# Linear attention and a gated long convolution on one core: the last output blocks sent one PSUM bank at a time over three queues, and the last 162 steps in a new order

## The chip, the cores and the metric

The kernel runs on one core of a Trainium2 chip. The metric is the device time of one execution in microseconds (us). Matrix products run on TensorE (PE, with PEld for its weight loads), elementwise work on VectorE (DVE), ScalarE (ACT) and GpSimd (POOL). The queues of SyncE (SP), ACT and POOL can issue DMAs, which sixteen DMA engines carry out.

## The reference

The inputs are q, k and v of 8 batches, 8 heads, 576 positions and 64 channels, a norm weight and three matrices. Linear attention without a softmax, an RMS norm per head, then a projection into three parts, of which the middle one is convolved over all 576 positions (as a product of spectra) and multiplied by the other two:

```python
kv  = einsum('bhsd,bhse->bhde', k, v)
out = einsum('bhsd,bhde->bhse', q, kv)
x   = out / sqrt(mean(out**2) + 1e-6) * g_norm      # heads side by side: 8 x 576 x 512
x1, x2, x3 = split(x @ w_proj, 3)
conv = irfft(rfft(x2) * rfft(filter))
return (x1 * conv * x3) @ w_out                     # 8 x 576 x 512, float32
```

## The kernel before, in words

Everything is written for a manual schedule. The work of one batch is cut into steps of a few instructions each, and a table of names, ORDER, lists all steps of all batches in one sequence; a name such as `Ga2.7` is step Ga2 of batch 7. Each engine executes its own instructions in the order in which the table lists them, and waits on the others by semaphores. There is no planner at run time: the table is the schedule.

PSUM is held as four pairs of banks. A step that writes PSUM takes a pair (or a single bank, `n=1`) by `take`, which picks the pair free for the longest, and the step that copies the result out gives it back by `free`.

For one batch b the steps are, in their order of dependence:

- K, O, sq, R, rs, ob or ov, x: the attention of a chunk of 128 channels (four chunks j = 0 to 3). O is the product on TensorE, sq its square on ACT, R the sum per head on TensorE, rs the reciprocal root on ACT, ob the copy with the weight (ov the same on VectorE), x their product on VectorE (line 543).
- eo, fa, fr, then abM, abT, rrM, rrT (lines 587 to 607) and eab, eT, err: sums and differences of positions on VectorE, the projection of the middle part on TensorE, and the copies on ACT (line 611).
- F0, F1t and F1, F2c and F2: the forward transform on TensorE (lines 629 to 656). M0, M1 (line 664) and M2 (line 679): the products with the filter's spectrum on VectorE. A0 and A1 (line 670): the sums of products, Y, on GpSimd; Av0 is A0 on VectorE.
- I01, I23, Io01, Io23: the inverse transform on TensorE (lines 718 and 719), copied out by ea, oa on ACT or ev, ov on VectorE (line 722), then vB and w on VectorE (lines 729 to 739).
- Ga0 to Ga3 and Gb0 to Gb3: the gates, the outer two parts of the projection, 8 matmuls each (line 689). x10 to x13 copy the first on ACT (line 695), g0 to g3 multiply the two on VectorE (line 697).
- fin: the product of gate and convolution on VectorE (line 742). For the last batch it goes in pieces: w and f with a first digit 0 or 1 for the first or second half of the positions and 01 or 23 for the chunks, so that `f123.7` is the second half of chunks 2 and 3.
- U0, U2: the output product, two blocks of 128 positions into a pair of banks, 8 matmuls (line 784). ot0, ot2: the copy of both blocks on ACT (line 788) and their sending on SP, by `send` (line 766), which cuts a block of 128 positions into two DMAs. U4, ot4: the block that two neighbouring batches share (lines 796 and 800). V0, V1: one block into a single bank (line 820), with va (ACT) or vv (VectorE) as the copy (line 826) and ds, dg, da as the sending on SP, POOL or ACT. Before the change only batch 7's blocks 0 and 1 go this way; ACT issues no DMA.

The table ends with the last gates of batch 7, U2 of batch 6, U2 of batch 7, V0, V1 and U4.

Of the kernel before, what the change touches and what calls it, by code (L numbers as in the profile page):

```python
# [46 lines left out]
M1.5 U2.3 ot2.3 Ga3.5 A1.5 x13.5 Gb3.5 O23.7 x.6 U0.4 sq2.7 g3.5 sq3.7 ov3.7 eo.6 Ga0.5 ob2.7 ot0.4 I23.5 Io23.5 x10.5  # L47
Io01.5 Gb0.5 ov23.5 oa01.5 ev23.5 I01.5 ea01.5 fa.6 g0.5 R2.7 Ga2.5 rs2.7 x12.5 abM.6 vB.5 abT.6 O01.7 eab.6 eT.6
Gb2.5 sq0.7 ob0.7 fr.6 w.5 rrM.6 sq1.7 g2.5 rrT.6 fin.5 F2c.6 ob1.7 F1t.6 F2.6 R1.7 err.6 M2.6 F1.6 U0.5 rs1.7 ot0.5
F0.6 Ga1.6 M1.6 R3.7 U2.5 x11.6 R0.7 M0.6 rs3.7 Ga2.6 U2.4 Av0.6 rs0.7 x0.7 A1.6 ot2.5 Gb2.6 x1.7 Io01.6 x12.6 eo.7  # L50
Gb1.6 g2.6 ot2.4 g1.6 Ga0.6 Io23.6 Gb0.6 oa01.6 oa23.6 I23.6 x10.6 I01.6 fa.7 ea23.6 ea01.6 abM.7 abT.7 Ga3.6 fr1.7
g0.6 eab.7 fr0.7 Gb3.6 vB.6 w.6 eT.7 rrM.7 x13.6 F2c.7 g3.6 rrT.7 F1t.7 F1.7 Ga0.7 err.7 fin.6 F2.7 F0.7 U4.5 M1.7
Ga1.7 x10.7 U0.6 x11.7 Gb1.7 M0.7 ot0.6 M2.7 Gb0.7 ot4.5 g1.7 A1.7 A0.7 g0.7 I01.7 Io01.7 Ga2.7 Io23.7 oa01.7 ev01.7
I23.7 oa23.7 Gb2.7 ea23.7 x12.7 Ga3.7 Gb3.7 vB01.7 vB23.7 g2.7 U2.6 w101.7 x13.7 ot2.6 g3.7 f101.7 w123.7 f123.7 U2.7
w023.7 ot2.7 w001.7 f023.7 f001.7 V0.7 V1a.7 V1b.7 U4.7 va1.7 va0.7 ds0.7 va4.7 dg1.7 ds4.7"""


@with_exitstack
def kernel(
# [11 lines left out]
    nc = tc.nc  # L71
    B, H, S, D = q.shape
# [4 lines left out]
    TH = S // 2  # L77
# [5 lines left out]
    lo, hi = slice(0, 64), slice(64, P)  # L83
    act, vec = nc.scalar, nc.vector
# [9 lines left out]
    held, tmp = {}, {}  # L94
# [63 lines left out]
    ind = consts.tile([P, P], BF16)  # L158
# [9 lines left out]
    g_col = consts.tile([P, 1], FP32)  # L168
# [10 lines left out]
    step = {}  # L179
# [278 lines left out]
    def qT(b):  # L458
        return buf("qT", b % 2, [P, H * 3, TR])
# [149 lines left out]
    def ev(name, key, o_, **kw):  # L609
        def f(b):  # L610
            act.copy(out=o_(), in_=tmp[key, b])  # L611
            free((key, b))
        step[name] = f

        def fv(b):
            vec.tensor_copy(out=o_(), in_=tmp[key, b])
            free((key, b))
        step["v" + name] = fv
# [138 lines left out]

    def send(q, b, at, ot):  # L760

        for i, x in enumerate([ot] if len(ot.shape) == 2 else [ot[:, 0], ot[:, 1]]):
            at_, p = at + i * P, 0
            while p < P:
                n = min(P - p, 96 - (at_ + p) % 96)
                q.dma_start(out=o_rows(b, at_ + p, n), in_=x[p:p + n])
# [8 lines left out]
    def ot_tile():  # L775
        turn[0] += 1
        return buf("ot", turn[0] % NOT, [P, 2, DM], FP32)

    def U(b, c0):
        pp = tmp['u', b, c0] = take(("u", b, c0))  # L780
        for cc in range(2):
            c = c0 + cc
            for dc in range(NDC):
                nc.tensor.matmul(pp[:, cc], ygt(b)[:, dc, b % 2 * 64 + c * P:b % 2 * 64 + (c + 1) * P], wo[:, dc], start=(dc == 0), stop=(dc == NDC - 1))  # L784

    def U_ev(b, c0, ev=act.copy):
        ot = ot_tile()
        ev(out=ot, in_=tmp['u', b, c0])  # L788
# [21 lines left out]
    step["ot4"] = U4_ev  # L810
    step["ov4r"] = lambda b: U4_ev(b, vec.tensor_copy)


# [12 lines left out]
        ev(out=ot, in_=tmp[k_])  # L826
# [54 lines left out]
```

## Time and profile before

| | us |
|---|---|
| median of three runs | 215.01 |
| lowest and highest | 214.27, 215.26 |
| profiled execution | 214.02 |
| span of the profiled execution | 212.2 |
| last result of TensorE, from the span's start | 205.7 |
| last issue of an output DMA starts | 208.0 |
| last bytes moved, by the slices of DMA activity, about | 210.4 |

Times in the trace count from the start of the span. A busy time is that in which an engine executed an instruction; for TensorE the matmuls overlap, so that the start of one piece of work to the start of the next is its pace. What stands in brackets is idle time before an instruction, with what ended it. The rows on DMA issues give pieces, their size and the median time from issue to landing.

### The profile page before, as it was taken

To read this page: it belongs to the slowest core of one execution; us is meant where nothing else is said; L and a number is where in the kernel's file an instruction comes from. 1 tells how busy PE (TensorE), PEld (TensorE's weight loads), DVE (VectorE), ACT (ScalarE), POOL (GpSimd) and SP (SyncE) were. 2 spreads that over 40 slices of the span, in tenths; PEclk is the share of its full clock that TensorE was granted. 3 is DMA by queue.
4 is the path that set the end of the run, shared out by engine and by line. 5 is a ranking of instruction groups with operands and counts; after the bars stand their busy time and mean duration, and the time that the engine had idled before them with its cause. 6 is when DMAs were issued, how large, how long until landed. Compare 5 with 4: busy or idle time off the path is not lost.

```text
span 212.2 us, 4930 instructions
## 1 busy us (share of the span) xinstructions
PE 200.7 (95%) x2014; PEld 120.8 (57%) x2014; DVE 183.1 (86%) x285; ACT 145.8 (69%) x240; POOL 58.8 (28%) x64
## 2 busy tenths in 40 slices
PE   3999999999999999999999999999999999999970
PEld 1454474466566666655667456665574567568620
DVE  6658997799999899899897999999999998998820
ACT  3649687768989996987689949474768565434450
POOL 8941140223741008301400067004500210044020
PEclk9999999999999999999999999999999999999997
DMA  3999999999999968999949209972330144004155
GB/s 29 200 205 206 207 207 205 204 173 174 203 203 204 204 127 107 181 248 251 213 127 153 60 3 152 285 83 64 99 102 0 34 127 140 3 2 110 38 169 179
DMA packets 37145, 30.14 MB, mean 142 GB/s; under 512 B 15906, under 2 KB 32290, under 8 KB 37122
## 3 DMA queue, kind: packets, MB, share of 16 engines
q0 software_dynamic: 17376, 17.11, 50.2%
q1 hardware_dynamic: 19746, 12.72, 26.1%
q8 instruction: 15, 0.25, 0.5%
q14 instruction: 8, 0.07, 0.1%
HBM read 33.69 MB, written 9.44 MB: 203 GB/s over the span
## 4 chain that ended last, share of the span: by engine, by line
PE 90%; DVE 3%; ACT 2%; issue 1%; POOL 1%; POOLq 0%; DVEq 0%
PE ps L689 29%; PE ps L784 12%; PE ps L601 7%; PE ps L112 6%; PE ps L718 5%; PE ps L515 3%; PE ps L587 3%; PE ps L607 3%; PE ps L436 3%; PE ps L508 3%; DVE tpw L664 2%; PE ps L594 2%; PE ps L645 2%; PE ps L631 2%; PE ps L373 1%; PE ps L719 1%
## 5 line engine op out<-in xcount | busy, mean ns | idle before, releaser
L689 PE MATMUL ps<-x,wp 128*128 128x288 bf16 x512 | 70.6, 286 | 0.1
L689 PEld LDWEIGHTS <-wp 128*128 128x128 bf16 x512 | 49.1, 98 | 16.7 <-issue 1.6
L670 POOL TENSOR_TENSOR Y<-tpw 128x1024 bf16<-128x1024 f32 (+1 forms) x11 | 28.0, 2549 | 73.5 <-DVE tpw L664 73.5
L664 DVE TENSOR_TENSOR tpw<-ps,HH 97x2048 f32<-97x2048 f32 (+1 forms) x16 | 36.4, 2286 | 2.3 <-PE ps L631 1.8
L784 PE MATMUL ps<-wo,yg 128*128 128x512 bf16 x120 | 28.4, 379 | 0.0
L697 DVE TENSOR_TENSOR g<-ps,x 128x576 bf16<-128x576 f32 x32 | 24.0, 754 | 5.1 <-PE ps L689 3.2
L695 ACT CAST x<-ps 128x576 bf16<-128x576 f32 x32 | 20.4, 641 | 9.3 <-PE ps L689 9.0
L528 ACT ACTIVATE rstd<-ps 128x576 bf16<-128x576 f32 x32 | 20.7, 656 | 7.2 <-PE ps L515 6.7
L788 ACT COPY ot<-ps 128x1024 f32<-128x1024 f32 x15 | 15.2, 1015 | 11.1 <-PE ps L784 11.0
L722 ACT CAST ar<-ps 128x576 bf16<-128x576 f32 x28 | 17.1, 645 | 7.9 <-PE ps L719 7.7
L611 ACT CAST x<-ps 128x1024 bf16<-128x1024 f32 (+1 forms) x20 | 17.2, 869 | 7.6 <-PE ps L601 3.3
L518 ACT ACTIVATE sq<-ps 128x576 bf16<-128x576 f32 x32 | 20.1, 654 | 3.4 <-PE ps L508 3.1
L524 ACT ACTIVATE o<-ps,g_col 128x576 bf16<-128x576 f32 x29 | 21.1, 750 | 0.0
L784 PEld LDWEIGHTS <-yg 128*128 128x128 bf16 x120 | 11.5, 98 | 12.9 <-issue 0.7
L112 PE MATMUL ps<-nil,ind 128*128 128x512 bf16 x42 | 13.9, 453 | 3.5 <-DVE ind L191 3.2
L718 PE MATMUL ps<-IV,Y 128*128 128x192 bf16 x128 | 15.7, 245 | 0.0
L601 PE MATMUL ps<-wp,ab 128*128 128x512 bf16 x64 | 15.1, 379 | 0.0
L515 PE MATMUL ps<-sq,ind 128*128 128x288 bf16 x64 | 12.9, 286 | 0.7 <-DVE tpw L664 0.5
L719 PE MATMUL ps<-IV,Y 97*128 97x96 bf16 x64 | 13.2, 207 | 0.0
L558 DVE TENSOR_TENSOR eo<-x 128x1152 bf16<-128x1152 bf16 (+1 forms) x18 | 12.2, 724 | 0.1
L742 DVE TENSOR_TENSOR yg<-w,g 128x576 bf16<-128x576 bf16 (+1 forms) x17 | 11.9, 718 | 0.2
L138 POOL DMA_DIRECT2D qb<-in_q_dram x11 | 8.3, 759 | 11.9 <-PE ps L478 9.4
(127 smaller groups left out, 293.3 us busy)
## 6 DMA issues: line engine op xcount, KB each, us to landing
out_dram<-ot SPq DMA_DIRECT2D x22, 192.0 KB, 3.2
vb<-in_v_dram POOLq DMA_DIRECT2D x7, 576.0 KB, 12.5
qb<-in_q_dram POOLq DMA_DIRECT2D x5, 576.0 KB, 13.4
kb<-in_k_dram POOLq DMA_DIRECT2D x5, 576.0 KB, 8.3
out_dram<-ot SPq DMA_DIRECT2D x22, 128.0 KB, 2.4
qb<-in_q_dram POOLq DMA_DIRECT2D x6, 288.0 KB, 8.6
kb<-in_k_dram POOLq DMA_DIRECT2D x6, 288.0 KB, 14.0
wp<-in_moe_w_proj_dram POOLq DMA_DIRECT2D x3, 512.0 KB, 17.0
```

The costliest lines, as they stand in the source:

```text
L112: nc.tensor.matmul(pair[i][:, j], ind, nil, start=True, stop=True)
L518: act.activation(out=halves(sq()[:, j]), in_=tmp['o', b, j][:, :, 0:TH], func=AF.Square)
L524: act.activation(out=halves(osb()[:, j]), in_=tmp['o', b, j][:, :, 0:TH], func=AF.Copy, scale=g_col)
L528: act.activation(out=halves(rstd()[:, j]), in_=tmp['r', b, j][:, :, 0:TH], func=AF.Abs_reciprocal_sqrt, scale=1.0 / D, bias=1e-6)
L601: nc.tensor.matmul(pp[:, h], abt()[:, j, 2 * h * P:(2 * h + 1) * P], w2(j), start=(j == 0), stop=(j == NDC - 1))
L664: vec.tensor_mul(out=t_[:n], in0=xp[:n].unsqueeze(1).to_broadcast([n, 2, 2, DM]), in1=two)
L670: op(out=Yt()[:n, 2 * g:2 * g + 2], in0=t_[:n, ::-1, 0], in1=t_[:n, ::-1, 1])
L689: nc.tensor.matmul(pp[:, h, 0:TH], w_, x[:, j, h * TH:(h + 1) * TH], start=(j == 0), stop=(j == NDC - 1))
L695: ev0(out=x1, in_=pp[:, :, 0:TH])
L697: vec.tensor_mul(out=halves(g13t()[:, dc]), in0=pp[:, :, 0:TH], in1=x1)
L718: nc.tensor.matmul(pp[:, i, 0:SB], Y[:, 2 * g + h, cs], IV[:, 2 * g + h, 0:SB], start=(g == 1), stop=(g == 2))
L784: nc.tensor.matmul(pp[:, cc], ygt(b)[:, dc, b % 2 * 64 + c * P:b % 2 * 64 + (c + 1) * P], wo[:, dc], start=(dc == 0), stop=(dc == NDC - 1))
```

## The change

The first 560 steps of the table stay as they are. The last 162 become 174 in another order, from `eo.6` on. No matmul is added or removed.

New steps: V2 and V3 (the existing V for blocks 2 and 3) replace U2 of batches 6 and 7, so that each of the four blocks has a bank of its own. `oc3.6` and `oh2.6` copy one such block on ACT and send its two parts on SP and ACT, or on SP and POOL. `va2`, `vv3`, `vv0`, `vv1` and `vv4` copy batch 7's blocks: four of the five on VectorE instead of ACT. `da2`, `dag3`, `ds1`, `dag0` and `dsa4` send them: both parts on ACT, on ACT and POOL, on SP, on ACT and POOL, on SP and ACT. `og0.4` and `og2.4` send U0 and U2 of batch 4 on POOL instead of SP. The inverse transform's copies ov23.5 and ev23.5 go from VectorE to ACT, ev01.7 becomes ea01.7 on ACT and oa23.7 becomes ov23.7 on VectorE. w.6 becomes four pieces, eo.7 two, and x0.7 and x1.7 become one x.7. Some of the functions that the diff adds (R2, e_rsw, e_xp, the steps op, os and sg, gs, sa, as, ga) are not listed in the table.

The core of the diff; of the table, its last line before and its last lines after:

```diff
-w023.7 ot2.7 w001.7 f023.7 f001.7 V0.7 V1a.7 V1b.7 U4.7 va1.7 va0.7 ds0.7 va4.7 dg1.7 ds4.7"""
+f123.7 V2.6 oc3.6 w001.7 w023.7 V2.7 f001.7 oh2.6 V3a.7 V3b.7 va2.7 f023.7 vv3.7 V0a.7 V0b.7 V1a.7 V1b.7 vv0.7 U4a.7
+U4b.7 vv1.7 da2.7 dag3.7 ds1.7 dag0.7 vv4.7 dsa4.7"""
...
-    def send(q, b, at, ot):
+    def send(qs, b, at, ot):
+        k = 0
...
-                q.dma_start(out=o_rows(b, at_ + p, n), in_=x[p:p + n])
+                qs[k % len(qs)].dma_start(out=o_rows(b, at_ + p, n), in_=x[p:p + n])
+                k += 1
...
+        step["og%d" % c0] = lambda b, c0=c0: U_ev(b, c0, qs=(nc.gpsimd,))
...
+    def V_row(b, c, qs):
+        ot = ot_tile()
+        act.copy(out=ot[:, 0], in_=tmp['v', b, c])
+        free(("v", b, c))
+        send(qs, b, b % 2 * 64 + c * P, ot[:, 0])
+
+    for c in range(4):
+        for e, qs in (("s", (nc.sync,)), ("c", (nc.sync, nc.scalar)), ("h", (nc.sync, nc.gpsimd))):
+            step["o%s%d" % (e, c)] = lambda b, c=c, qs=qs: V_row(b, c, qs)
...
+        queues = {"s": nc.sync, "g": nc.gpsimd, "a": nc.scalar}
+        for e in ("s", "g", "a", "sg", "gs", "sa", "as", "ga", "ag"):
+            step["d%s%d" % (e, c)] = lambda b, c=c, e=e: V_out(b, c, [queues[x] for x in e])
```

Three places in the order of the instructions. First the end of SP's queue before, where ot_1364 holds U2 of batch 6, ot_1403 U2 of batch 7, kb0_70 V0 and sq_105 U4:

```order
L766 DMA out_0_dram<-ot_1364 32x512
L766 DMA out_0_dram<-ot_1364 96x512 x2
L766 DMA out_0_dram<-ot_1364 32x512
L766 DMA out_0_dram<-ot_1403 64x512 x2
L766 DMA out_0_dram<-ot_1403 32x512
L766 DMA out_0_dram<-ot_1403 96x512
L766 DMA out_0_dram<-kb0_70 32x512
L766 DMA out_0_dram<-kb0_70 96x512
L766 DMA out_0_dram<-sq_105 64x512 x2
```

and the same end after (the line is 794 there), where ot_1364 holds V3 of batch 6, ot_1403 V2 of batch 6 and kb1_71 V1 of batch 7:

```order
L794 DMA out_0_dram<-ot_1364 96x512
L794 DMA out_0_dram<-ot_1403 32x512
L794 DMA out_0_dram<-kb1_71 96x512
L794 DMA out_0_dram<-kb1_71 32x512
L794 DMA out_0_dram<-sq_105 64x512
```

SP issued twelve parts of the last blocks and now issues five; of the fourteen, six go to ACT and three to POOL (two were on POOL before).

Second the end of ACT's queue before, where the last five rows are the copies of U2 of batches 6 and 7, V1, V0 and U4:

```order
L695 CAST x1_116<-ps_3_69 128x576
L695 CAST x1_119<-ps_1_67 128x576
L788 COPY ot_1364<-ps_3_69 128x1024
L788 COPY ot_1403<-ps_0_66 128x1024
L826 COPY kb1_71<-ps_3_69 128x512
L826 COPY kb0_70<-ps_1_67 128x512
L826 COPY sq_105<-ps_2_68 128x512
```

and after, where line 866 copies V3 and V2 of batch 6, line 858 V2 of batch 7 (vb0_72), and vb1_73 and kb0_70 hold V3 and V0 of batch 7:

```order
L722 CAST x1_119<-ps_3_69 128x576
L722 CAST x1_116<-ps_0_66 128x576
L866 COPY ot_1364<-ps_2_68 128x512
L794 DMA out_0_dram<-ot_1364 32x512
L866 COPY ot_1403<-ps_0_66 128x512
L858 COPY vb0_72<-ps_1_67 128x512
L794 DMA out_0_dram<-vb0_72 64x512 x2
L794 DMA out_0_dram<-vb1_73 32x512
L794 DMA out_0_dram<-kb0_70 32x512
L794 DMA out_0_dram<-sq_105 64x512
```

ACT copies three single banks where it copied seven banks in five instructions, and issues six DMAs, four of them behind other engines' copies.

Third the end of VectorE's queue before, with the last two gate products (line 697), the pieces of w (lines 737 and 739) and of the final product (line 742):

```order
L697 TENSOR_TENSOR g13_111<-ps_0_66,x1_116 128x576
L739 TENSOR_TENSOR w_113<-bb_102 128x2x288
L697 TENSOR_TENSOR g13_111<-ps_2_68,x1_119 128x576
L742 TENSOR_TENSOR yg_103<-w_113,g13_111 128x2x288
L739 TENSOR_TENSOR w_113<-bb_102 128x2x288
L742 TENSOR_TENSOR yg_103<-w_113,g13_111 128x2x288
L737 TENSOR_TENSOR w_113<-bb_102 128x2x288 x2
L742 TENSOR_TENSOR yg_103<-w_113,g13_111 128x2x288 x2
```

and after, where the same steps have the lines 724, 764, 766 and 769:

```order
L766 TENSOR_TENSOR w_113<-bb_102 128x2x288 x2
L724 TENSOR_TENSOR g13_111<-ps_1_67,x1_119 128x576
L769 TENSOR_TENSOR yg_103<-w_113,g13_111 128x2x288
L724 TENSOR_TENSOR g13_111<-ps_3_69,x1_116 128x576
L769 TENSOR_TENSOR yg_103<-w_113,g13_111 128x2x288
L764 TENSOR_TENSOR w_113<-bb_102 128x2x288 x2
L769 TENSOR_TENSOR yg_103<-w_113,g13_111 128x2x288 x2
L858 COPY vb1_73<-ps_3_69 128x512
L858 COPY kb0_70<-ps_2_68 128x512
L858 COPY kb1_71<-ps_0_66 128x512
L858 COPY sq_105<-ps_1_67 128x512
```

Both pieces of w's second half now stand ahead of the gate products, and the copies of V3, V0, V1 and U4 stand at the end, where VectorE had nothing. On TensorE the last gates are Gb3, Ga3, then V3 of batch 6, then Ga2, Gb2, then V2 of batch 6, V2, V3, V0, V1 and U4 of batch 7; before, they were Ga2 among the inverse transform, Gb2, Ga3, Gb3, then U2 of batch 6, U2 of batch 7, V0, V1 and U4.

More of the change, by code (lines that the diff above doesn't have):

```diff
@@ L46 @@
 abT.5 eT.5 abM.5 x11.5 fin.4 eab.5 M0.5 R1.6 Gb1.5 rs1.6 K.7 F1t.5 g1.5 F2c.5 eKv.7 F2.5 M2.5 R0.6 F1.5 A0.5 rs0.6
[L47 to L54, printed above, removed]
-w023.7 ot2.7 w001.7 f023.7 f001.7 V0.7 V1a.7 V1b.7 U4.7 va1.7 va0.7 ds0.7 va4.7 dg1.7 ds4.7"""
+M1.5 U2.3 ot2.3 Ga3.5 A1.5 x13.5 Gb3.5 O23.7 x.6 U0.4 sq2.7 g3.5 sq3.7 ov3.7 ob2.7 og0.4 Ga2.5 R3.7 eo.6 x12.5 I01.5
+fa.6 rs3.7 Io01.5 fr.6 Gb2.5 oa01.5 ea01.5 I23.5 ea23.5 g2.5 Io23.5 oa23.5 abM.6 eab.6 abT.6 Ga0.5 vB.5 O01.7 eT.6
+x10.5 w.5 Gb0.5 rrM.6 rrT.6 sq0.7 sq1.7 g0.5 ob1.7 F2c.6 F1t.6 ob0.7 err.6 fin.5 F2.6 Ga2.6 M2.6 x12.6 F1.6 R1.7 rs1.7
+U0.5 M1.6 A1.6 R0.7 ot0.5 F0.6 rs0.7 Ga1.6 x11.6 U2.5 M0.6 R2.7 U2.4 rs2.7 Av0.6 ot2.5 Gb1.6 og2.4 I23.6 Io23.6 Gb2.6
+x.7 oa23.6 eo0.7 eo1.7 g1.6 ea23.6 Ga0.6 I01.6 Gb0.6 g2.6 fa.7 x10.6 fr0.7 Io01.6 fr1.7 ea01.6 Ga3.6 oa01.6 g0.6 abM.7
+Gb3.6 vB.6 abT.7 x13.6 w001.6 eab.7 eT.7 rrM.7 w123.6 F2c.7 w023.6 g3.6 rrT.7 w101.6 F1t.7 F1.7 U4.5 err.7 Ga1.7 ot4.5
+fin.6 M1.7 F0.7 F2.7 x11.7 M0.7 A1.7 Ga0.7 U0.6 Gb0.7 x10.7 ot0.6 M2.7 A0.7 g0.7 Gb1.7 I01.7 Io23.7 g1.7 ea01.7 ov23.7
+Io01.7 oa01.7 I23.7 ea23.7 Gb3.7 vB01.7 vB23.7 Ga3.7 x13.7 w101.7 V3.6 Ga2.7 w123.7 x12.7 Gb2.7 g3.7 f101.7 g2.7
+f123.7 V2.6 oc3.6 w001.7 w023.7 V2.7 f001.7 oh2.6 V3a.7 V3b.7 va2.7 f023.7 vv3.7 V0a.7 V0b.7 V1a.7 V1b.7 vv0.7 U4a.7
+U4b.7 vv1.7 da2.7 dag3.7 ds1.7 dag0.7 vv4.7 dsa4.7"""
 @with_exitstack
@@ L515, in R, with R2, e_rsw @@
             nc.tensor.matmul(r2[:, h, 0:TH], ind, sq()[:, j, h * TH:(h + 1) * TH], start=True, stop=True)
+    def R2(b, j):
+        rr = [take(("r", b, j + i)) for i in range(2)]
+        for i in range(2):
+            tmp['r', b, j + i] = rr[i]
+        for h in range(2):
+            for i in range(2):
+                for p, q in ((lo, hi), (hi, lo)):
+                    nc.tensor.matmul(rr[i][q if i else p, h, 0:TH], ind[p, p], sq()[p, j + i, h * TH:(h + 1) * TH], start=True, stop=True)
+    def e_rsw(b, j):
+        act.activation(out=halves(sq()[:, j]), in_=tmp['r', b, j][:, :, 0:TH], func=AF.Abs_reciprocal_sqrt, scale=1.0 / D, bias=1e-6)
+        free(("r", b, j))
+        for p, q in ((lo, hi), (hi, lo)):
+            nc.sync.dma_start(out=rstd()[q, j], in_=sq()[p, j])
     def e_sq(b, j):
@@ L525, in e_o, with e_xp @@
         free(("o", b, j))
+    def e_xp(b, j):
+        vec.scalar_tensor_tensor(out=halves(xt(b)[:, j]), in0=tmp['o', b, j][:, :, 0:TH], scalar=g_col, in1=halves(rstd()[:, j]),
+                                 op0=ALU.mult, op1=ALU.mult)
+        free(("o", b, j))
     def e_rs(b, j):
@@ L532 @@
         step["O%d" % j] = lambda b, j=j: O(b, j)
+        step["xp%d" % j] = lambda b, j=j: e_xp(b, j)
         step["R%d" % j] = lambda b, j=j: R(b, j)
         step["rs%d" % j] = lambda b, j=j: e_rs(b, j)
+        step["rsw%d" % j] = lambda b, j=j: e_rsw(b, j)
+        if j % 2 == 0:
+            step["Rq%d%d" % (j, j + 1)] = lambda b, j=j: R2(b, j)
         step["sq%d" % j] = lambda b, j=j: e_sq(b, j)
@@ L784, in U, with U_ev @@
                 nc.tensor.matmul(pp[:, cc], ygt(b)[:, dc, b % 2 * 64 + c * P:b % 2 * 64 + (c + 1) * P], wo[:, dc], start=(dc == 0), stop=(dc == NDC - 1))
-    def U_ev(b, c0, ev=act.copy):
+    def U_ev(b, c0, ev=act.copy, qs=(nc.sync,)):
         ot = ot_tile()
@@ L789, in U_ev @@
         free(("u", b, c0))
-        send(nc.sync, b, b % 2 * 64 + c0 * P, ot)
+        send(qs, b, b % 2 * 64 + c0 * P, ot)
     def U4(b, d0, d1):
@@ L796, in U4, with U4_ev @@
             nc.tensor.matmul(tmp['u4', b], yg4()[:, b // 2 % 2, dc, 4 * P:5 * P], wo[:, dc], start=(dc == 0), stop=(dc == NDC - 1))
-    def U4_ev(b, ev=act.copy):
+    def U4_ev(b, ev=act.copy, qs=(nc.sync,)):
         ot = ot_tile()
@@ L801, in U4_ev @@
         free(("u4", b))
-        send(nc.sync, b - 1, 4 * P, ot[:, 0])
+        send(qs, b - 1, 4 * P, ot[:, 0])
     for c0 in (0, 2):
@@ L806 @@
         step["ot%d" % c0] = lambda b, c0=c0: U_ev(b, c0)
+        step["op%d" % c0] = lambda b, c0=c0: U_ev(b, c0, qs=(nc.sync, nc.gpsimd))
+        step["og%d" % c0] = lambda b, c0=c0: U_ev(b, c0, qs=(nc.gpsimd,))
         step["ov%dr" % c0] = lambda b, c0=c0: U_ev(b, c0, vec.tensor_copy)
@@ L810 @@
     step["ot4"] = U4_ev
+    step["op4"] = lambda b: U4_ev(b, qs=(nc.sync, nc.gpsimd))
     step["ov4r"] = lambda b: U4_ev(b, vec.tensor_copy)
@@ L827, in V_ev, with V_out @@
         free(k_)
-    def V_out(b, key, q):
-        send(q, *((b - 1, 4 * P) if key == 4 else (b, b % 2 * 64 + key * P)), tmp['ot', b, key])
+    def V_out(b, key, qs):
+        send(qs, *((b - 1, 4 * P) if key == 4 else (b, b % 2 * 64 + key * P)), tmp['ot', b, key])
+    def V_row(b, c, qs):
[6 more added lines that the diff above has]
+            step["o%s%d" % (e, c)] = lambda b, c=c, qs=qs: V_row(b, c, qs)
     for c in range(5):
```

2 lines of the change are left out of this document (removed).

## The prediction

> **What bounds the kernel now.** I read the page's busy times first, then the stretches of time at the end of the span, then the chain of waits there, and last the DMA issues.
>
> ```profile
> PE 200.7 (95%) x2014; PEld 120.8 (57%) x2014; DVE 183.1 (86%) x285; ACT 145.8 (69%) x240; POOL 58.8 (28%) x64
> ```
>
> In the stretches the columns are busy us of PE, PEld, DVE, ACT and POOL, then clock, DMA share and GB/s.
>
> ```profile
> 190.00:200.00 10.00, 10.00 (x85) 7.47 (x84) 8.18 (x16) 5.14 (x8) 3.46 (x2) 1.00 0.30 79
> 200.00:206.00 6.00, 5.66 (x25) 2.07 (x23) 2.81 (x8) 3.19 (x5) 0.28 (x1) 1.00 0.42 119
> 206.00:212.20 6.20, 0.00 (x0) 0.00 (x0) 0.00 (x0) 0.40 (x1) 0.78 (x2) 0.80 0.60 182
> ```
>
> TensorE is full up to its last matmul, at full clock, and the change removes no matmul. Then come more than 6 us in which only outputs leave. So a gain can come from two places: gaps inside TensorE's queue, and the tail. The chain of waits shows the gaps (start, us, what):
>
> ```profile
> 189.98 1.73 PE ps L784 x8
> 196.34 2.94 PE ps L689 x24
> 199.28 3.62 PE ps L784 x16
> 202.90 1.91 PE ps L820 x8
> ```
>
> Eight matmuls of 512 columns run in 1.73, 0.216 each. Sixteen should take 3.46 and took 3.62; the eight of V took 1.91. These gaps, 0.16 and 0.18, are all that the end of the queue has to give. The last result, the four of U4, comes at 204.81 + 0.87 = 205.68.
>
> The tail in order of time, ACT's copies and the issues on SP and POOL:
>
> ```profile
> 201.04 1.01 ACT L788 COPY ot<-ps 128x1024 f32<-128x1024 f32 x1 [2.01 <-PE ps L784]
> 202.93 1.01 ACT L788 COPY ot<-ps 128x1024 f32<-128x1024 f32 x1 [0.88 <-PE ps L784]
> 204.84 1.07 ACT L826 COPY kb<-ps 128x512 f32<-128x512 f32 x2 [0.90 <-PE ps L820]
> 205.80 0.60 ACT L826 COPY sq<-ps 128x512 f32<-128x512 f32 x1
> 202.08 3.00 SPq L766 DMA_DIRECT2D out_dram<-ot  x6
> 205.72 1.06 POOL L766 DMA_DIRECT2D out_dram<-kb  x2 [12.26 <-ACT kb L826]
> 206.34 1.05 SPq L766 DMA_DIRECT2D out_dram<-kb  x2
> 207.49 1.25 SPq L766 DMA_DIRECT2D out_dram<-sq  x2
> 208.01 0.74 SPq L766 DMA_DIRECT2D out_dram<-sq  x1
> out_dram<-sq SPq DMA_DIRECT2D x1, 128.0 KB, 3.1
> ```
>
> U4's copy is done at 206.40, but SP is still busy with earlier pieces, so the last piece is issued at 208.01, 1.6 late. It lands 3.1 later, at 211.1; the span ends 1.1 after that. The DMA engines are the second thing to look at:
>
> ```profile
> 202.00:203.00 1.00, 0.99 (x6) 0.30 (x4) 0.84 (x3) 0.12 (x2) 0.00 (x0) 1.00 0.09 23
> 205.00:206.00 1.00, 0.66 (x4) 0.10 (x1) 0.00 (x0) 1.00 (x3) 0.28 (x1) 1.00 0.81 197
> 207.00:208.00 1.00, 0.00 (x0) 0.00 (x0) 0.00 (x0) 0.00 (x0) 0.00 (x0) 1.00 1.02 311
> 205.40:210.40 5.00, 0.26 (x2) 0.00 (x0) 0.00 (x0) 1.00 (x3) 1.06 (x2) 0.93 0.84 248
> ```
>
> The seven banks of the end (4 of U2, then V0, V1, U4) are 7 x 256 KB = 1.84 MB. They start to move at about 202.9, 0.8 after the first issue, and at 248 GB/s need 7.4 us, to about 210.4. SP's issues and the engines' drain are late together.
>
> **The change: TensorE's part.** The number of matmuls is the same. One bank of batch 6 (V3.6, 4 x 0.216 = 0.87) now stands ahead of the last two gates, so the last gate's result comes at 199.28 + 0.87 = 200.15 instead of 199.28. VectorE then needs the gate product and one half of the final product:
>
> ```profile
> 199.38 0.76 DVE L697 TENSOR_TENSOR g<-ps,x 128x576 bf16<-128x576 f32 x1
> 200.91 0.46 DVE L742 TENSOR_TENSOR yg<-w,g 128x576 bf16<-128x576 bf16 x1
> 201.29 0.82 DVE L737 TENSOR_TENSOR w<-bb 128x576 bf16<-128x576 bf16 x2
> 202.02 0.82 DVE L742 TENSOR_TENSOR yg<-w,g 128x576 bf16<-128x576 bf16 x2
> ```
>
> That is 200.15 + 0.10 + 0.76 + 0.46, with small handovers about 201.55. TensorE has V2.6 (0.87) and the first half of V2.7 (0.43) to do, to 201.45, and waits 0.15. The other four VectorE pieces (1.55 from 201.29 to 202.84) now end at 203.1; V3.7 runs to 202.9, the first half of V0 needs only f001 (done about 202.7) and the second is wanted at 203.35: covered. So the gaps of 0.34 become 0.15.
>
> Upstream one handover has no slack: the sums Y of batch 7 before the inverse transform.
>
> ```profile
> 187.54 0.60 PE L631 MATMUL ps<-x,FX 128*97 128x512 bf16 x2
> 186.39 4.49 DVE L664 TENSOR_TENSOR tpw<-ps,HH 128x2048 f32<-128x2048 f32 x2 [0.36 <-PE ps L645]
> 188.76 4.70 POOL L670 TENSOR_TENSOR Y<-tpw 128x1024 bf16<-128x1024 f32 x2 [18.14 <-DVE tpw L664]
> 193.50 0.33 PE L718 MATMUL ps<-IV,Y 128*128 128x192 bf16 x2
> ```
>
> GpSimd ends its second sum at 193.46 and TensorE wants it at about 193.6. F0.7 now follows F1.7 by U4.5 and a gate (0.87 + 0.98) instead of a gate and one matmul (0.98 + 0.22), 0.65 later: it ends at 188.8 instead of 188.14, and the second product of VectorE, free at 188.63, starts 0.25 later. GpSimd was itself busy to 191.1, so its second sum ends some 0.15 later and TensorE waits about 0.1. TensorE's end: -0.34 + 0.15 + 0.1, about -0.1, with bounds of -0.3 (no waits left) and +0.5 (these waits three times as long).
>
> The other moves of the 162 steps I cost at nothing, since VectorE and the gates' matmuls cover them:
>
> ```profile
> 150.00:160.00 10.00, 10.00 (x85) 6.66 (x83) 9.96 (x15) 6.76 (x11) 3.40 (x1) 1.00 0.39 105
> 155.39 1.41 DVE L722 CAST ar<-ps 128x576 bf16<-128x576 f32 x2
> 171.62 1.43 DVE L543 TENSOR_TENSOR x<-o,rstd 128x1152 bf16<-128x1152 bf16 x2
> 176.71 1.02 DVE L564 TENSOR_TENSOR ab<-eo 128x768 bf16<-128x768 bf16 x2
> 179.06 1.89 PE L601 MATMUL ps<-wp,ab 128*128 128x512 bf16 x8
> 182.05 0.76 DVE L737 TENSOR_TENSOR w<-bb 128x1152 bf16<-128x1152 bf16 x1
> ```
>
> VectorE is full from 150 to 160, but loses two casts there (ov23.5 and ev23.5, 1.41, now on ACT, which is at 6.76 of 10). The four pieces of w.6 cost 4 x 0.41 against 2 x 0.75, 0.15 more. R2.7 is moved behind U2.5, so x.7, now one piece that needs all four chunks, starts some 0.9 later than x0.7 did; its last reader fa.7 ended 1.3 before abM.7, and abM.7 itself moves back behind a gate (0.98). If that cover failed it would cost the 0.9. GpSimd's eight new issues, 0.54 each, stand ahead of sums before which it idles (18.14 us before the last pair).
>
> **The tail.** The nearest row to VectorE's new copies:
>
> ```profile
> L616 DVE CAST x<-ps 128x512 bf16<-128x512 f32 x1 | 0.7, 685 | 0.0
> L766 SPq DMA_DIRECT2D out_dram<-ot x66: 315/452/1466, 70.0 to 205.8; - x66
> L766 POOL DMA_DIRECT2D out_dram<-kb x2: 517/536/554, 205.7 to 206.3; - x2
> ```
>
> U4's result at 205.6, the copy 0.69, done at 206.35; V1's copy ends at 205.45 and its two pieces hold SP for 2 x 0.45, to 206.4. Then SP and ACT issue one piece of U4 each: the last issue at 206.4 instead of 208.01, **-1.6**, if it lands 3.1 later as now.
>
> The drain says how much of that counts. Pieces start to move 0.8 after issue. V3.6 is copied by ACT behind the gate's copy (about 200.4) and moves from 201.2; V2.6 from 202.5; V2.7 (two issues on ACT) from 203.5; V3.7, V0 and V1 from 204.6, 205.4, 206.2; U4 from 207.2. At 248 GB/s a bank takes 1.06, so from the second on they follow each other without a gap and the last ends at 202.5 + 6 x 1.06 = 208.9 instead of 210.4: **-1.5**. At 197 GB/s (1.33 a bank) the last ends at 210.5: nothing won. At 311 (0.84) it ends at about 208.05, 0.84 after U4 starts: -2.35. I take 248, the mean of the whole tail; the drain and the issues then agree.
>
> The Trainium skill, page "DMA: Bandwidth & Descriptors", section "Issuing engines are not separate DMA queues", speaks against the change: all queues run on the same 16 engines, and several issuers save only the time of issuing. By that rule the rate would not rise, and rival A below would set the time; the trace leans half that way, with 0.84 busy, but 1.02 and 311 GB/s in the one slice in which POOL's pieces move beside SP's.
>
> **Sum**: -0.1 and -1.5, so -1.6. The profiled execution took 214.02 (span 212.2 and 1.8 around it) and would take 212.4. The median of the runs is 215.01, so I forecast 213.4.
>
> **The rivals.**
> A. *The drain binds.* The engines were at 0.8 already; smaller steps from three queues do not raise the rate, and at 197 to 225 GB/s (between the worst slice and the mean) the last bank ends 0 to 0.8 earlier. 214.2 to 215.0. For: the slice at 197 with 0.81 busy. Against: the slice at 311.
> B. *The engines fill better.* With two or three queues the slice at 311 GB/s is the rule: -2.35 and -0.1, 212.6. Against: U4's pieces alone cannot move before 207.2.
> C. *ACT's issues are dear* (the other side). ACT issued no DMA before; in the tail it issues six pieces, the last of U4. At SP's dearest, 1.47, the first, ahead of ACT's copies of V2 of both batches, pushes the end of those to 203.1, and of the other five the last starts at 203.1 + 4 x 1.47 = 209.0, 1.0 later than now: 216.0. It decides from 1.35 a piece on, where the last would start at 208.0. Against: SP's median is 0.45.
> D. *The Y chain stretches.* If GpSimd's two sums ran as slowly as its slowest in the row below (3.40 instead of 2.35), TensorE would wait 2.1 more before the inverse transform and lose the whole gain: 215.5. Against: VectorE's work beside them is the same as before, and they kept to 2.35.
>
> ```profile
> 150.78 3.40 POOL L670 TENSOR_TENSOR Y<-tpw 128x1024 bf16<-128x1024 f32 x1 [2.98 <-DVE tpw L664]
> ```
>
> **How the numbers follow.** Forecast 0.55, A 0.19, B 0.14, C 0.07, D 0.05. Anything within 0.5%, 1.1 us, is what a measurement of this kernel cannot tell from no change. Faster by more: B, and the forecast but for its slow edge (0.03 of it), 0.66. Slower by more: of C the 0.05 in which a piece costs over 1.5 (nothing bounds it from above here), of D the 0.02 in which the tail gives nothing either, 0.07. The rest, 0.27, is the same. The forecast's own range is 212.8 to 214.2 (drain between 225 and 275 GB/s, TensorE's bounds). The range given reaches down past B to 212.2 and up over A to 215.1; it leaves out C, D and the ends.
>
> **What would show it.** TensorE's last matmul within 0.4 of 205.6 and no wait over 0.3 before L745 or L852; U4's copy on DVE about 0.69 long; the last issue within 1.0 us of TensorE's end (2.3 before); the rate of the tail at 248 or more; the span's end about 1.1 after the last landing. ACT issues above 1.3 us, a rate near 200, or a gap of over 1 us on TensorE after 150 would make it wrong.

## The result and the profile after

| us | before | changed |
|---|---|---|
| median (lowest to highest, 7 runs each) | 214.67 (213.98 to 215.26) | 213.31 (212.90 to 214.39) |
| profiled execution, span | 214.02, 212.2 | 213.31, 211.5 |
| U0.4 starts on TensorE | 151.45 | 151.64 |
| U0.4 to TensorE's last result | 54.22 | 54.47 |
| TensorE's last result to the end of the span | 6.53 | 5.39 |

The ratio is 0.9944 [0.9918, 0.997]: faster by 0.3 to 0.8%, 1.36 us between the medians. U0.4 is the last step on TensorE that stands at the same place in both tables, so the fourth row is the time that TensorE needs for the reordered part (the last result is the start of U4's four matmuls and 1.03). In these two profiles all that is won lies behind TensorE's end: 1.14. TensorE itself became 0.25 slower.

The page of the changed kernel, engines and the queue that ACT now has:

```profile
PE 201.0 (95%) x2014; PEld 121.0 (57%) x2014; DVE 185.0 (87%) x290; ACT 145.2 (69%) x240; POOL 63.4 (30%) x73
...
q10 hardware_dynamic: 384, 0.59, 1.0%
```

Its tail in order of time, the issues on ACT, then SP and POOL:

```profile
200.29 0.59 ACT L866 COPY ot<-ps 128x512 f32<-128x512 f32 x1
200.91 0.40 ACTq L794 DMA_DIRECT2D out_dram<-ot  x1
203.31 1.82 ACTq L794 DMA_DIRECT2D out_dram<-vb  x3
205.23 1.18 ACTq L794 DMA_DIRECT2D out_dram<-kb  x1
206.87 0.50 ACTq L794 DMA_DIRECT2D out_dram<-sq  x1
206.00 0.79 SPq L794 DMA_DIRECT2D out_dram<-kb  x2
206.89 0.71 SPq L794 DMA_DIRECT2D out_dram<-sq  x1
205.41 0.51 POOL L794 DMA_DIRECT2D out_dram<-kb  x1 [0.35 <-DVE kb L858]
206.15 0.69 DVE L858 COPY sq<-ps 128x512 f32<-128x512 f32 x1 [0.17 <-PE ps L825]
```

Three of ACT's six issues send what VectorE copied (vb1, kb0 and sq), not four as said of the order of the instructions; the two from vb0 stand behind ACT's own copy.

U4's copy starts 0.04 after TensorE's last result (206.11), takes 0.69 on VectorE, and both of its pieces are issued 0.05 later: the last issue starts 0.78 after TensorE's end, where it was 2.3. The landings of the last pieces, however, have become longer (issues by tile, KB, us to landing):

```profile
out_dram<-kb POOLq DMA_DIRECT2D x1, 192.0 KB, 4.1
out_dram<-sq ACTq DMA_DIRECT2D x1, 128.0 KB, 3.2
out_dram<-sq SPq DMA_DIRECT2D x1, 128.0 KB, 3.5
```

3.5 instead of 3.1 for the last. In stretches of time, the last three columns being clock, DMA share and GB/s:

```profile
203.00:204.00 1.00, 1.00 (x6) 0.41 (x5) 0.91 (x3) 0.28 (x1) 0.11 (x1) 1.00 0.62 164
204.00:205.00 1.00, 1.00 (x6) 0.49 (x5) 0.83 (x2) 0.00 (x0) 0.46 (x1) 1.00 0.65 197
206.00:207.00 1.00, 0.11 (x1) 0.00 (x0) 0.69 (x1) 0.00 (x0) 0.00 (x0) 1.00 0.86 273
208.00:209.00 1.00, 0.00 (x0) 0.00 (x0) 0.00 (x0) 0.00 (x0) 0.00 (x0) 1.00 0.89 275
```

From 203 to 205 the DMA engines have a third of their time to spare. From 205 to 209 they are at 0.86 to 0.95, and the data end at about 209.7.

The 0.25 on TensorE is a wait ahead of the inverse transform. The sums and products of batch 7 (F0 is L656 and L658, the products L691, GpSimd's sums L697):

```profile
186.50 2.29 DVE L691 TENSOR_TENSOR tpw<-ps,HH 128x2048 f32<-128x2048 f32 x1 [0.65 <-PE ps L672]
188.29 0.59 PE L658 MATMUL ps<-x,FX 128*97 128x512 bf16 x2
188.73 0.38 PE L683 MATMUL ps<-x,FZ 128*128 128x512 bf16 x1
189.37 2.29 DVE L691 TENSOR_TENSOR tpw<-ps,HH 97x2048 f32<-97x2048 f32 x1 [0.58 <-PE ps L683]
191.74 2.35 POOL L697 TENSOR_TENSOR Y<-tpw 97x1024 bf16<-97x1024 f32 x1 [0.51 <-DVE tpw L691]
193.68 0.33 PE L745 MATMUL ps<-IV,Y 128*128 128x192 bf16 x2
194.16 0.22 PE L746 MATMUL ps<-IV,Y 97*128 97x96 bf16 x1 [0.15 <-POOL Y L697]
```

Before, the two products stood back to back, and the two sums too. Now VectorE stands idle for 0.58 between them and GpSimd for 0.51. The first L746 starts 0.48 after L745 instead of 0.16: 0.32 lost.

### The profile page after: what moved, and what is told of

It reads as the page before. It is cut to its first block, busy times and chain, and to the rows that moved or that the text cites. A ratio compares the mean times of both kernels' runs of the same rounds, so it can differ in the third digit from the quotient of the medians.

```text
span 211.5 us, 4941 instructions
## 1 busy us (share of the span) xinstructions
PE 201.0 (95%) x2014; PEld 121.0 (57%) x2014; DVE 185.0 (87%) x290; ACT 145.2 (69%) x240; POOL 63.4 (30%) x73
## 4 chain that ended last, share of the span: by engine, by line
PE 87%; DVE 5%; POOL 3%; ACT 2%; issue 1%; DVEq 0%; POOLq 0%
PE ps L716 27%; PE ps L813 10%; PE ps L628 7%; PE ps L113 6%; PE ps L745 5%; PE ps L516 3%; PE ps L614 3%; DVE tpw L691 3%; PE ps L634 3%; PE ps L437 3%; PE ps L509 3%; POOL Y L697 2%; PE ps L621 2%; PE ps L852 2%; PE ps L672 2%; PE ps L658 1%
## 5 line engine op out<-in xcount | busy, mean ns | idle before, releaser
L697 POOL TENSOR_TENSOR Y<-tpw 128x1024 bf16<-128x1024 f32 (+1 forms) x11 | 28.0, 2544 | 65.5 <-DVE tpw L691 65.5
L691 DVE TENSOR_TENSOR tpw<-ps,HH 97x2048 f32<-97x2048 f32 (+1 forms) x16 | 36.6, 2288 | 4.0 <-PE ps L658 2.3
L813 PE MATMUL ps<-wo,yg 128*128 128x512 bf16 x104 | 24.6, 380 | 0.0
L749 ACT CAST ar<-ps 128x576 bf16<-128x576 f32 x30 | 18.2, 646 | 5.7 <-PE ps L746 5.5
L817 ACT COPY ot<-ps 128x1024 f32<-128x1024 f32 x13 | 13.2, 1016 | 7.4 <-PE ps L813 7.3
L813 PEld LDWEIGHTS <-yg 128*128 128x128 bf16 x104 | 10.0, 98 | 10.8 <-issue 0.7
L745 PE MATMUL ps<-IV,Y 128*128 128x192 bf16 x128 | 15.7, 246 | 0.0
L746 PE MATMUL ps<-IV,Y 97*128 97x96 bf16 x64 | 13.3, 207 | 0.2 <-POOL Y L697 0.2
```

The source lines that it names most:

```text
L691: vec.tensor_mul(out=t_[:n], in0=xp[:n].unsqueeze(1).to_broadcast([n, 2, 2, DM]), in1=two)
L697: op(out=Yt()[:n, 2 * g:2 * g + 2], in0=t_[:n, ::-1, 0], in1=t_[:n, ::-1, 1])
L745: nc.tensor.matmul(pp[:, i, 0:SB], Y[:, 2 * g + h, cs], IV[:, 2 * g + h, 0:SB], start=(g == 1), stop=(g == 2))
```

## The experiments

In the tables of steps below, "middle" is what lies between `eo.6` and `I01.7`, the first step of batch 7's inverse transform, and "tail" what follows it.

**One half at a time.** The table was cut at I01.7 and the halves of the two kernels joined crosswise.

```diff
-(middle of the changed kernel) I01.7 (tail of the changed kernel)
+(middle of the kernel before)  I01.7 (tail of the changed kernel)   # old middle, new tail
+(middle of the changed kernel) I01.7 (tail of the kernel before)    # new middle, old tail
```

> The order before up to the inverse transform of batch 7, then the changed tail (single banks, three queues, copies on VectorE). Tail theory (the whole gain is made behind the inverse transform; the new middle order costs the wait of 0.32 us before it): TensorE does not wait before the inverse transform, the stretch from TensorE's last result to the span's end is about 5.4 us as in the changed kernel (6.5 before), and the time is 1.3 to 1.7 us under the kernel before, so at or a little below the changed one. Order theory (the new middle order wins time too): no more than 0.7 us under the kernel before, 0.5 or more slower than the changed one.

> The changed order up to the inverse transform of batch 7, then the tail of before (pairs of banks, copies on ACT, twelve parts on SP). Tail theory: the wait before the inverse transform is there (0.3 us), the stretch behind TensorE's last result is 6.5 us again, the time is 0 to 0.5 us above the kernel before. Order theory: 0.5 or more under the kernel before.

Old middle, new tail: 213.08, ratio 0.9934 [0.992, 0.9948]. New middle, old tail: 214.66, ratio 1.0008 [0.9992, 1.0024]. So the whole gain belongs to the tail. In the traces, U0.4 to TensorE's last result and the rest of the span are 54.15 and 5.39 in the first, 54.50 and 6.74 in the second: the new middle adds a third of a microsecond, the new tail takes more than one away.

**F0 back where it was.** Only the steps between F1.7 and I01.7 take the order of before.

```diff
-F1.7 U4.5 err.7 Ga1.7 ot4.5 fin.6 M1.7 F0.7 F2.7 x11.7 M0.7 ...
+F1.7 Ga0.7 err.7 fin.6 F2.7 F0.7 U4.5 M1.7 Ga1.7 x10.7 U0.6 x11.7 Gb1.7 M0.7 ...
```

> The changed kernel, but with the 20 steps between F1.7 and the inverse transform in their order of before, so that F0.7 follows F1.7 by a gate and one matmul again and F2.7 stands ahead of it. If F0.7's place is the cause of the wait, the second product on VectorE starts within 0.1 us of the end of the first, GpSimd's second sum ends 0.5 to 0.6 us earlier and TensorE's wait before the inverse transform goes: 0.3 to 0.5 us under the changed kernel. If the wait comes from the steps further up (VectorE later as a whole), it stays and the time is the changed kernel's.

212.90, ratio 0.9927 [0.9913, 0.9941]. Products and sums are back to back again:

```profile
186.35 4.50 DVE L691 TENSOR_TENSOR tpw<-ps,HH 128x2048 f32<-128x2048 f32 x2 [0.66 <-PE ps L672]
188.73 4.68 POOL L697 TENSOR_TENSOR Y<-tpw 128x1024 bf16<-128x1024 f32 x2 [11.77 <-DVE tpw L691]
```

and U0.4 to the last result takes 54.09 instead of 54.47. The wait and its place are shown. What it is worth at the end of the span is another question, for which both kernels ran once more on one chip (below).

**F2 ahead of F0.** This asks whether the second product waits for F0 or for F2's matmul behind it.

```diff
-M1.7 F0.7 F2.7 x11.7 M0.7
+M1.7 F2.7 F0.7 x11.7 M0.7
```

> The changed kernel with F2.7 and F0.7 exchanged on TensorE and nothing else. In the changed kernel VectorE's second product starts 0.49 us behind F0.7's last matmul and 0.26 behind F2.7's, which the profile names as what it waited for. If it waits for whichever of the two comes last, then F0.7, now last (0.22 later), is followed by the product after 0.1 to 0.3 us: it starts at about the same time as now or up to 0.15 earlier. If there is a fixed 0.49 behind F0.7, it starts 0.2 later than now and TensorE waits 0.2 more before the inverse transform.

```profile
187.88 0.38 PE L683 MATMUL ps<-x,FZ 128*128 128x512 bf16 x1
188.32 0.59 PE L658 MATMUL ps<-x,FX 128*97 128x512 bf16 x2
189.38 2.29 DVE L691 TENSOR_TENSOR tpw<-ps,HH 97x2048 f32<-97x2048 f32 x1 [0.78 <-PE ps L658]
```

The product starts 0.47 after F0's last matmul (188.91), as against 0.49 in the changed kernel (188.88 to 189.37) and 0.47 in its second profile. It is F0 that is waited for, wherever F2 stands, and here F0 is itself 0.2 later (one execution; 213.61, and U0.4 to the last result 54.67). But this handover, from the last matmul to the start of the product, is long. The same pair of lines earlier in the trace of the changed kernel takes 0.10:

```profile
103.00 0.60 PE L658 MATMUL ps<-x,FX 128*97 128x512 bf16 x2
103.70 2.29 DVE L691 TENSOR_TENSOR tpw<-ps,HH 97x2048 f32<-97x2048 f32 x1 [0.43 <-PE ps L658]
```

What holds the product for the other 0.37 is not settled; ends of matmuls are modelled in the profile, and no run took it apart.

**All pieces on SP.** The order and the copies of the changed kernel, but one queue for the last seven banks.

```diff
-oc3.6 ... oh2.6 ... da2.7 dag3.7 ds1.7 dag0.7 vv4.7 dsa4.7
+os3.6 ... os2.6 ... ds2.7 ds3.7 ds1.7 ds0.7 vv4.7 ds4.7
```

> The changed kernel with all fourteen parts of the last seven banks sent by SP. Issue theory (the queue held the last part back): SP needs 14 x 0.45 us from about 200.9, issues U4's second part some 0.5 to 0.7 us later than in the changed kernel, and the time is 0.5 to 0.7 us above it. Drain theory (the sixteen DMA engines hold the end, three queues add nothing): U4's last part is issued later but lands at the same time, the time is the changed kernel's within 0.2.

213.60, ratio 0.9966 [0.9953, 0.9978]; the rest of the span behind TensorE's end is 6.03.

```profile
203.16 2.92 SPq L794 DMA_DIRECT2D out_dram<-vb  x4
206.18 1.82 SPq L794 DMA_DIRECT2D out_dram<-kb  x4
208.09 1.11 SPq L794 DMA_DIRECT2D out_dram<-sq  x2
```

Ten issues, most of them 0.4 to 0.6 long and one 1.24, hold SP for 6.0 us with no pause over 0.1, and U4's pieces go out at 208.09, 1.4 after their copy; but they land in 2.4. Of the 1.14 that the tail won, single banks and VectorE's copies alone give 0.50 (6.53 to 6.03), and three queues add 0.64 (6.03 to 5.39). These are single profiles, and two profiles of one program can differ by more (below). The medians of the set show the order but not the split: 214.38 before and 213.60 with one queue; the two kernels with three queues, 213.08 and 212.90, also lack the third of a microsecond that the new middle costs. The changed kernel itself did not run in this set; its ratios in two others, 0.9944 and 0.9929, lie 0.2 to 0.4% under the 0.9966 here, with intervals that overlap or nearly touch. The Trainium skill, page "DMA: Bandwidth & Descriptors", section "Issuing engines are not separate DMA queues", allows several issuers only the time of issuing, usually small beside the transfer. Here that time was not small: 6.0 us for the last five banks, which at 249 GB/s (below) take 5.3 to move.

**Only the queues divided.** The kernel before, its order and ACT's copies kept, with the last parts on three queues.

```diff
-ot2.6 ... ot2.7 ... va0.7 ds0.7 va4.7 dg1.7 ds4.7
+op2.6 ... op2.7 ... va0.7 dsa0.7 va4.7 dag1.7 dsa4.7
```

> The kernel before with only the sending of its last seven banks divided: U2 of batches 6 and 7 on SP and POOL, V0, V1 and U4 on SP and ACT, POOL and ACT, SP and ACT; copies and order as before. Issue theory: U4's parts are issued at 206.5 instead of 207.5 and 208.0, the stretch behind TensorE's last result falls from 6.5 to about 5.9 us, the time by 0.6. Drain theory: the engines have 1.84 MB to move from 202.9 on and are done at 210.3 whoever issues; landing takes 1 to 1.5 us longer, the time is that of the kernel before within 0.3.

214.39, ratio 0.9999 [0.9983, 1.0015]: nothing.

```profile
205.15 1.07 ACT L857 COPY kb<-ps 128x512 f32<-128x512 f32 x2 [0.90 <-PE ps L851]
206.26 0.40 ACTq L793 DMA_DIRECT2D out_dram<-kb  x1
207.04 0.58 ACT L857 COPY sq<-ps 128x512 f32<-128x512 f32 x1 [0.81 <-ACT kb L857]
207.66 0.75 ACTq L793 DMA_DIRECT2D out_dram<-sq  x1
out_dram<-sq ACTq DMA_DIRECT2D x1, 128.0 KB, 3.9
```

U4's result is there at 205.98, but ACT copies it only at 207.04. Of the 0.81 of idle time before this copy its own issue takes 0.40; what the rest waited for is not shown. Even so the last issue starts 1.68 after TensorE's last result instead of 2.33. What is won there is lost in the landing, 3.9 instead of 3.1, and the drain as a whole tells why. The stretches in which the last seven banks moved, before, with only the queues divided, and in the changed kernel (ends read from slices of 0.25; in the second a few packets follow to 211.1):

```profile
202.85:210.40 7.55, 2.81 (x13) 1.09 (x12) 0.00 (x0) 2.58 (x4) 1.06 (x2) 0.96 0.82 243
203.15:210.75 7.60, 2.82 (x13) 1.09 (x12) 0.01 (x1) 2.67 (x4) 2.13 (x5) 0.99 0.82 240
201.70:209.70 8.00, 4.29 (x20) 1.68 (x18) 4.54 (x9) 1.17 (x2) 1.54 (x3) 1.00 0.79 232
```

With only the queues divided the bytes begin 2.8 ahead of TensorE's last result, as before, and take as long, as the drain theory had it. In the changed kernel they take 8.0, but begin 4.4 ahead, since V3 and V2 of batch 6 go out as single banks: 1.6 earlier less 0.45 longer is the 1.14 of the tail. So with more queues alone the drain was as late and as long as before, and nothing was won. What ACT's delayed copy cost besides is not shown.

**Half of the bytes.** The changed kernel, but of the last seven banks only the first 256 of the 512 columns are sent; the other half of these rows is not written.

```diff
-                qs[k % len(qs)].dma_start(out=o_rows(b, at_ + p, n), in_=x[p:p + n])
+                m = DM // 2 if 'half' in tmp else DM
+                qs[k % len(qs)].dma_start(out=o_rows(b, at_ + p, n, m), in_=x[p:p + n, 0:m])
```

> The changed kernel, but the last seven banks send only the first 256 of their 512 columns (half of the bytes, as many parts and rows; half of these rows of the output is not written). Drain theory: the last parts land 2.0 to 2.5 us after their issue instead of 3.2 to 3.5, and the span ends 0.9 to 1.2 us earlier behind TensorE's last result (4.3 instead of 5.4). If landing is a fixed time that does not hang on the bytes, the end moves by less than 0.3.

211.95, ratio 0.9883 [0.9861, 0.9904], 1.0 to 1.4 below the two medians of the changed kernel (212.92 and 213.31). The last issue still starts 0.77 after TensorE's end, but its landing and the stretch behind it are:

```profile
out_dram<-sq SPq DMA_DIRECT2D x1, 64.0 KB, 2.0
```

```profile
207.00:208.00 1.00, 0.00 (x0) 0.00 (x0) 0.00 (x0) 0.00 (x0) 0.00 (x0) 1.00 0.53 160
```

The rest of the span falls from 5.39 to 4.22, and the DMA engines are half idle. So in the changed kernel the drain, not the issues, sets the end.

**V3 sent earlier.** On top of F0 put back: V3 of batch 6 copied ahead of the gate's copy x12.7, sent by SP alone, or by SP and ACT.

```diff
-V3.6 Ga2.7 w123.7 x12.7 Gb2.7 g3.7 f101.7 g2.7 f123.7 V2.6 oc3.6 w001.7
+V3.6 Ga2.7 w123.7 os3.6 x12.7 Gb2.7 g3.7 f101.7 g2.7 f123.7 V2.6 w001.7   # SP alone
+V3.6 Ga2.7 w123.7 oc3.6 x12.7 Gb2.7 g3.7 f101.7 g2.7 f123.7 V2.6 w001.7   # SP and ACT
```

> The kernel with F0.7 back in its place, and V3 of batch 6 copied by ACT ahead of the gate's copy x12.7 and sent by SP, some 1.5 us earlier than now (its result waits on ACT's order). Drain theory: one bank of the seven is moved in the time in which the DMA engines idle, so the last parts meet a shorter line and land up to 0.9 us sooner: 0.4 to 0.9 us under that kernel without this step. Issue theory: U4's last part is issued at the same time and nothing changes (within 0.2).

SP alone: 213.31, ratio 0.9945 [0.9927, 0.9964], nothing won, and 6.35 behind TensorE's end in its profile. In the view by queue (slices of 0.25 us) ACT's first data of this run move from about 204.1, 1.5 after the issue at 202.55. That made a theory of ACT's queue, for which SP and ACT were tried, beside the changed kernel and the one with F0 put back, all three on one chip:

> V3 of batch 6 copied ahead of x12.7, as in the run before in which SP alone sent it, but with its two parts on SP and ACT again. Theory (the first DMA that ACT's queue carries starts to move 1.35 to 1.6 us after its issue, where SP's takes 0.8; in the run with SP alone this first use fell on batch 7's block 2, whose data moved only from 204.0 while the DMA engines were idle): with ACT's queue used from about 198.9, block 2's data follow their issue by about 1.1, the DMA engines are busy from 203.5 on, and with one bank of seven gone from the end the tail is 5.51 less up to 0.9, about 4.8 to 5.3: 212.2 to 212.7. Rival (an early block gives the end nothing, or costs it, whichever queue it takes; the drain of the last six banks is what counts): tail 5.5 to 6.3, 212.9 to 213.3.

> The kernel with the changed tail and the old order of the steps between F1.7 and I01.7 once more, beside the changed kernel itself on the same chip. Theory (the new order there costs a wait of about 0.3 before the inverse transform and nothing else): 0.3 to 0.4 under the changed kernel, 212.9. Rival (the 0.4 between them was the chip's, from one set of runs to the next): no difference, 213.3.

> The changed kernel once more, as the base of the other two runs. If nothing but the chip differs, 213.3, a ratio of about 0.994 to the kernel before; TensorE's end 54.5 after the start of U0.4, the tail 5.4.

| | median | ratio to before | U0.4 to last result | rest of the span |
|---|---|---|---|---|
| V3 early, SP and ACT | 212.93 | 0.9922 [0.9898, 0.9946] | 54.08 | 5.07 |
| F0 put back | 212.98 | 0.9922 [0.9898, 0.9945] | 54.09 | 6.72 |
| changed | 212.92 | 0.9929 [0.9908, 0.9949] | 54.45 | 5.30 |

The profile with V3 early came out as its theory said, at 5.07, but the medians are the same: the theory falls as a statement on time. The DMA engines say why an earlier V3 gives nothing: from 202 to 204 they were at 0.60 and 0.64 even so, waiting for data, and the backlog that sets the end builds up only afterwards, from the last five banks. F0's 0.36 on TensorE is there again (54.45 against 54.09), yet no median shows it: it is less than intervals of about 0.5 to either side can tell apart. No version tried is shown to beat the changed kernel.

The 6.72 is the lesson of this set. The same program had 5.52 in its first profile. Issues stand at the same distance from TensorE's end in both; the landings do not. The second profile of the kernel with F0 put back:

```profile
out_dram<-kb POOLq DMA_DIRECT2D x1, 192.0 KB, 4.8
out_dram<-sq SPq DMA_DIRECT2D x1, 128.0 KB, 4.8
```

```profile
208.00:209.00 1.00, 0.00 (x0) 0.00 (x0) 0.00 (x0) 0.00 (x0) 0.00 (x0) 0.50 0.67 215
209.00:210.00 1.00, 0.00 (x0) 0.00 (x0) 0.00 (x0) 0.00 (x0) 0.00 (x0) 0.50 0.13 47
210.00:211.00 1.00, 0.00 (x0) 0.00 (x0) 0.00 (x0) 0.00 (x0) 0.00 (x0) 0.50 0.03 10
```

and its first, one line of the same view:

```profile
209.00:210.00 1.00, 0.00 (x0) 0.00 (x0) 0.00 (x0) 0.00 (x0) 0.00 (x0) 0.96 0.04 14
```

In one execution most of the sixteen engines are done at 209 and a few packets dribble on to 210.4; in the other all are done at 209.2. That execution took 213.88, the longest of its six (212.54 to 213.88). So one profile gives the tail to about a microsecond only. The 6.35 with V3 on SP alone looks different: there the DMA engines were at 0.42 and 0.57 in the two slices from 203 to 205 (0.77 and 0.82 in the first profile with F0 put back), two of ACT's issues took 0.94 and 1.49, and the data ran on to about 209.8 without a dribble. Why ACT's queue was late there is not shown.

## Why the prediction was right, and where it was not

**Time and sign.** 213.31 against 213.4; the gain is 1.36 between the medians, against 1.6. That the time came out within 0.1 is in part luck: the forecast started from 215.01, the median of three runs, and seven runs gave 214.67, so a base 0.34 too high and a gain 0.24 too large nearly cancel. The two profiled executions differ by 0.71 only, as the one before was on the quick side of its runs (214.02 of 213.98 to 215.26) and U0.4 started 0.19 later in the one after.

**TensorE, -0.1.** It was +0.25; this step failed, within its bounds of -0.3 to +0.5. It had two parts. The gaps at the end should have gone from 0.34 to 0.15. The chain of waits of the changed kernel shows the wait at V2.7 where it was put:

```profile
200.75 0.77 DVE g L724
201.51 0.02 issue
201.54 0.47 DVE yg L769
202.01 0.05 issue
202.05 3.19 PE ps L852 x14
```

From the end of the gate (200.65) to 202.05 are 1.40, for which the prediction had 0.10 + 0.76 + 0.46 and handovers, and TensorE has 1.30 of work. The 20 matmuls from 200.48 to U4's first at 205.08 take 4.60 where 20 x 0.216 is 4.32, so 0.28 remains of the gaps, not 0.15. This part is -0.06; with F0 put back, which leaves it alone, the whole is -0.13 (54.22 to 54.09). The other part, "TensorE waits about 0.1" before the inverse transform, measured 0.32. The cause was named rightly, F0 moved behind U4.5 and a gate; what failed is "starts 0.25 later". F0 ended at 188.88, near the 188.8 worked out, but VectorE did not start at once: with the handover of 0.49 the idle time was 0.58, GpSimd's second sum ended at 194.09 instead of 193.46, and of the 0.63 there 0.19 is the later start of U0.4 and 0.44 the chain, where 0.15 was forecast.

**Tail, -1.5.** It was -1.14. The step on the issues held: the copy took 0.69 as estimated, and the last issue came 0.78 after TensorE's last result, as worked out (205.6 to 206.4). "If it lands 3.1 later as now" did not: it landed 3.5 later, and these 0.4 are the difference between -1.5 and -1.14. The step on the drain failed in "from the second on they follow each other without a gap". V2.7 was to move from 203.5, so to be issued at about 202.7. ACT issued it at 203.31, 0.6 later, of which TensorE's lateness is about 0.5; and its data moved from about 204.4, 1.1 behind the issue, where the sum has 0.8 for every piece. The engines were at 0.62 and 0.65 until then. From 204.4 five banks at 1.06 give 209.7, which is where the data ended: the rate of 248 was right, its start was not. Two stretches of the changed kernel:

```profile
204.00:209.70 5.70, 2.11 (x10) 0.78 (x8) 2.32 (x4) 0.00 (x0) 1.02 (x2) 1.00 0.83 249
206.12:209.70 3.58, 0.00 (x0) 0.00 (x0) 0.69 (x1) 0.00 (x0) 0.00 (x0) 1.00 0.85 270
```

**The rivals.** A, the drain binds: right as a mechanism, as half of the bytes showed (1.0 to 1.4 us), wrong as a price, since the engines moved 249 over the whole stretch and not 197 to 225. B, 311 GB/s throughout: not seen; 270 from 206.12 to 209.70. C, ACT's issues are dear: of the six in the changed kernel five took 0.40 to 0.61 and one 1.18, none 1.35. With F0 put back and with V3 on SP alone one issue took 1.55 and 1.49, over the 1.35, but only one: the last issue came 0.78 and 1.21 after TensorE's last result, where C needs 2.3 or more. An issue does push back the copy behind it, by 0.81 when only the queues were divided. In the changed kernel this is 0.17: V2 of batch 6 is copied 1.24 after its first matmul starts (200.48 to 201.72), and 1.07 after it with all pieces on SP. D, the Y chain: the place was right, the sums kept to 2.36 and 2.35; the wait came from VectorE. That the middle's other moves cost nothing is in accord with the runs: new middle, old tail is at 1.0008, and U0.4 to the last result is 0.28 higher there, which the wait of 0.32 covers.

**What was to show it.** The last result came at 206.11, 0.5 late where 0.4 was allowed: 0.19 is the later start of U0.4, the rest the failed term. The wait before the inverse transform was 0.32 where 0.3 was allowed, from the same term. Copy, last issue, rate and the 1.1 from the last landing (206.89 + 3.5) to the end came as named.

## What to carry to other kernels

A tail of outputs has three clocks: when the last result is copied, when the last piece is issued, when the bytes are through. Taking one away pays up to the next only. Here queues alone gave nothing, with the drain as late and as long as before; single banks, copies and order on one queue gave 0.5 and all together 1.1 in the profiles, and then the drain stood there. When a step is moved so that an engine has to wait for it, cost the handover too, not only the lateness of the step: it was hidden while the two stood back to back. And a tail read from one profile of each kernel is good to about a microsecond; what is below that is for medians on one chip.

## What the runs showed of the hardware

- ACT's queue started later than SP's. SP's data moved about 0.8 after the issue (198.54 to about 199.35 with V3 early). ACT's first data moved 1.4 to 1.5 after it (198.55 to about 199.95, beside SP's data, and 202.55 to about 204.1, with no data moving just before), and later ones about 1.1 (202.53 to about 203.65), read in slices of 0.25.
- ACT stood idle for 0.81 before a copy behind an issue when only the queues were divided, 0.40 of it the issue itself; in the changed kernel a copy began 0.81 after the start of an issue (200.91 to 201.72). It is not always so: with V3 early on both queues the gate's copy started at 198.98, 0.03 after the end of the issue (198.55 and 0.40).
- An issue is not always the 0.4 to 0.6 that most take: one in ten on SP took 1.24, one in six on ACT 1.18, with the data there. In the other profiles with three queues the longest of ACT's took 0.88 to 1.55.
- Behind a backlog U4's pieces of 128 KB took 2.9 to 4.8 us to land; with one queue, issued 1.3 later behind TensorE's last result, 2.4; with half of the bytes, 2.0 to 2.2.
